# Attention scores issued as four 64x64 quarters of TensorE, with keys kept in half tiles

## The chip, the core and the metric

The kernel runs on one NeuronCore of one Trainium2 chip. The metric is the device time of one execution in microseconds (us). PE is the matrix engine TensorE, PEld its weight loads, DVE the vector engine, ACT the scalar engine, POOL the GpSimd engine and SP the engine whose queue issues nearly all DMAs. ns are nanoseconds.

## What is computed

An attention layer with a causal window of 128 keys, a token-mixing and channel-mixing layer, and a normalized feed-forward layer, for 4 sequences of 576 positions and 8 heads of 64. Cut to what the change touches:

```python
# B, H, S, D = 4, 8, 576, 64
scores = scale * np.matmul(q, k.transpose(0, 1, 3, 2))
rel = pos[:, None] - pos[None, :]
bias = slopes[:, None, None] * (-np.abs(rel))[None, :, :]
mask = (rel >= 0) & (rel < 128)
scores = np.where(mask, scores + bias[None], -1e9)
attn = softmax(scores)
x = attn @ v
# then, per sequence: u = x + (relu(x^T w_tok1) w_tok2)^T
#                     u = u + relu(u w_ch1) w_ch2
#                     out = u + relu(layernorm(u) w_ch1') w_ch2'
```

A query sees itself and the 127 keys before it. So a tile of 128 queries needs two tiles of keys, its own and the one before; 64 queries need only 192 keys.

## The kernel before

The 2304 positions are cut into 18 tiles of 128. Tile `i` may begin a sequence (tiles 0 and 9), and then it has one tile of keys; the 16 others have two. All operations are handed to `Plan.op` with a cost in ns for each engine that may run them, the tiles read and the tiles written. `Plan.order` (L205) is a list scheduler: it plays these costs through and fixes the order of every engine's instructions, SP's DMAs among them. A changed cost or an added operation can therefore move others, far from it.

**Attention (`attention`, L747).** In iteration `i` of the loop the block of `packed(i + 1, i - 1)` (L578) is issued on PE: first the scores of tile `i + 1`, in two parts `c` of four heads, then the products of the probabilities of tile `i - 1` with the values (`ps_v`, L608). The four parts are chained, so that nothing comes between them. Scores (L596) are fp32 matmuls: the stationary operand is 64 rows (one head's depth) of `q` by 128 queries, the moving one the 256 keys of the two key tiles. Heads come in pairs `j`, whose depths lie in partitions 0 to 63 and 64 to 127, and whose results go to two different PSUM banks of `ps_s`. Each fp32 matmul leaves two records in the trace, so a block of 8 score matmuls has 16 records; the 16 value matmuls have 32.

**Keys** lie in `keys`, a ring of RING = 4 tiles (L524); a load of 256 KB fills one (L532). For tiles whose place is the ring's first, the tile before is the ring's last, and `keys_of` (L563) gives a slice with a step that takes places 0 and 3 in turn, own keys first.

**Softmax (`softmax`, L623).** On DVE one `copy_predicated` (L631) of 128 x 512 takes, for each query, the older key's score wherever the own tile's key lies after the query, so that 128 columns are left of 256. Then four reductions (`CUSTOM_DVE_ANT_0`, L637) add the bias and find the minimum `mn`. ACT takes the exponentials (`pr`, L646), PE transposes them (`ps_t`, L653), ACT copies them to `pf` (L361), and POOL's `affine_select` (L663) splits them into the two key tiles. `normalize` (L667) has ACT copy `ps_v` to `ut`, PE transpose it and DVE scale it into `u[i]`.

**What runs beside it.** The token-mixing weights come as 64-bit floats through one buffer `rh` and two buffers `rw` (L404) and are made into fp32 pairs: `e` on ACT (L416), `s`, `m` and `y` on DVE (L419 to L431). `tok1` and `tok2` (L440 to L442, L735 to L737) are the token-mixing matmuls in three fp32r products each. They fill PE between the blocks. Near the end of attention `prep_wide` (L859) transposes `u` (`p`, L848) and lets DVE, ACT and POOL form sums and differences (`st`) and high and low halves (`xh`, `xl`) for the channel-mixing layer, whose first products are L993 to L995. From about 190 us on that layer and the next keep PE busy to the end.

Of the kernel before, what the change touches and what calls it, by code (L numbers as in the profile page):

```python
# [10 lines left out]
F32 = mybir.dt.float32  # L11
# [3 lines left out]
I32 = mybir.dt.int32  # L15
# [8 lines left out]
B, H, S, D = 4, 8, 576, 64  # L24
P = 128
DM = H * D
NT = B * S
NTILE = NT // P
# [4 lines left out]
RING = 4  # L33
# [69 lines left out]
class Plan:  # L103
# [22 lines left out]
    def buf(self, pool, shape, dtype, tag, bufs=1):  # L126
        b = Buf(self, pool, shape, dtype, tag, bufs)
        ring = self.rings.setdefault((pool, tag), [])
        if len(ring) >= bufs:
            b.after = [ring[-bufs]]  # L130
        if ring:
            b.behind = ring[-1]
        ring.append(b)
        return b
# [176 lines left out]
def pe(n):  # L311
    return 2.6 + n / 2.4


def block_kernel(tc, qT, kT, v, wt1, wt2, wa1, wa2, wb1, wb2, g, bias, out):
# [5 lines left out]
    def op(cost, emit, reads=(), writes=(), behind=()):  # L321
        return pl.op(cost, (lambda e: emit()) if len(cost) == 1 else emit, reads, writes, behind)
# [198 lines left out]
        return [buf("hid", [P, 2, S + P], F32R, "few" + p) for p in "hl"]  # L521


    keys = buf("att", [P, RING, H // 2, P], F32, "keys")  # L524
    wt1h, wt1l = ([buf("tok", [P, 5, TOK], F32R, f"wt1{x}{odd}") for odd in range(2)] for x in "hl")
    wt2h, wt2l = few()
    vs, qs = {}, {}
# [1 line left out]
    def load_qk(i):  # L529
        r = i % RING  # L530
        b = qs[i] = buf("att", [P, H // 2, P], F32, "q", Q_BUFS)
        op({"DMA": 1000}, lambda: nc.sync.dma_start(out=keys.t[:, r].rearrange("p h t -> p (h t)"), in_=kT[i]),  # L532
           writes=[(keys, r)])
        load(b, lambda: b.t.rearrange("p h t -> p (h t)"), P * DM * 4, qT[i])

    def load_v(i):
# [25 lines left out]

    def keys_of(i):  # L563

        s = i % RING
        if starts_batch(i):
            return [i], 0, 0, (s, s + 1, 1)
        table = 3 if len(batches_of(i)) > 1 else 2 if len(batches_of(i - 1)) > 1 else 1
        if s == 0:
            return [i, i - 1], 0, table, (0, RING, RING - 1)  # L570
        return [i - 1, i], 1, table, (s - 1, s + 1, 1)

    pv = buf("psb", [P, H // 2, P], F32, "ps_v")
    rs_t, xh_t, xl_t = {}, {}, {}
# [3 lines left out]
    def packed(i, i2):  # L578

        parts, ready = [], []
        if i is not None:
            tiles, own, table, (a0, a1, a2) = keys_of(i)
            w = len(tiles) * P
            x = qs[i]
            for c in range(2):
                ps_t[i, c] = buf("psa", [P, 2, 2, 2 * P], F32, "ps_s", 2)  # L590

                def scores(c=c, ps=ps_t[i, c]):
                    for p in range(2):
                        for j in range(2):
                            r = slice(j * D, (j + 1) * D)
                            nc.tensor.matmul(ps.t[:, j, p, :w], x.t[r, 2 * c + p], keys.t[r, a0:a1:a2, 2 * c + p],  # L596
                                             start=True, stop=True)

                parts.append((4 * pe(2 * w), scores, [x] + [(keys, t % RING) for t in tiles], [ps_t[i, c]]))
        if i2 is not None:  # L600
            tiles2 = keys_of(i2)[0]
            na = len(tiles2)
            for c in range(2):
                def values(c=c, pf=pf_t[i2, c]):
                    for p in range(2):
                        for a, kt in enumerate((i2, i2 - 1)[:na]):
                            for j in range(2):
                                nc.tensor.matmul(pv.t[j * D:(j + 1) * D, 2 * c + p], vs[kt].t[:, 4 * c + 2 * p + j],  # L608
                                                 pf.t[:, a, 2 * p + j], start=(a == 0), stop=(a == na - 1))

                parts.append((na * 440, values, [(pf_t[i2, c], a) for a in range(na)] + [vs[kt] for kt in tiles2],
                              [(pv, c)]))

        before = None
        for k, (cost, emit, reads, writes) in enumerate(parts):
            also = parts[k + 1:] if k == 0 else []
            now = op({"PE": cost + (200 if k in (0, len(parts) - 1) else 0)}, emit,
               reads + [x for p in also for x in p[2]], writes + [x for p in also for x in p[3]])
            if before is not None:
                pl.chain[before] = now  # L620
            before = now

    def softmax(i, c):  # L623

        tiles, own, table, _ = keys_of(i)
        na = len(tiles)
        ps = ps_t[i, c]
        o = slice(own * P, (own + 1) * P)
        if na == 2:
            b = slice((1 - own) * P, (2 - own) * P)  # L630
            op({"DVE": 690}, lambda: nc.vector.copy_predicated(  # L631
                ps.t[:, :, :, o], after.t.bitcast(I32).unsqueeze(1).unsqueeze(1).to_broadcast([P, 2, 2, P]),
                ps.t[:, :, :, b]), [ps, after], [ps])
        t = buf("att", [P, 4, P], F32, "t", T_BUFS)
        mn = buf("small", [P, 4], F32, "mn", 3)
        for m in range(4):
            op({"DVE": 358}, lambda m=m: nc.vector.tensor_tensor_reduce(  # L637
                out=t.t[:, m], in0=ps.t[:, m % 2, m // 2, o], in1=bias_sb.t[:, table, 4 * c + m],
                scale=-0.125, scalar=3.0e38, op0=ALU.add, op1=ALU.min, accum_out=mn.t[:, m:m + 1]),
               [ps, (bias_sb, table)], [(t, m), (mn, m)])  # L640
        pr = buf("att", [P, 4, P], F32, "pr", T_BUFS)
        if c == 0:
            rs_t[i] = buf("small", [P, H, 1], F32, "rs", 3)
        rs = rs_t[i]
        for m in range(4):
            op({"ACT": 580}, lambda m=m: nc.scalar.activation(  # L646
                out=pr.t[:, m], in_=t.t[:, m], func=AF.Exp, bias=mn.t[:, m:m + 1], scale=-1.0,
                accum_out=rs.t[:, 4 * c + m]), [(t, m), (mn, m)], [(pr, m), (rs, 4 * c + m)])
        pt = buf("psb", [P, 4, P], F32, "ps_t")

        def transposes():
            for m in range(4):
                nc.tensor.transpose(pt.t[:, m], pr.t[:, m], ident.t)  # L653

# [558 lines left out]
```

## Time and profile before

| | |
|---|---|
| time, median of 3 | 854.13 us (853.57 to 858.12) |
| the profiled execution | 856.19 us, of which its span is 854.5 us |
| PE busy in the span | 830.8 us (97%) |
| DVE busy | 638.1 us (75%) |
| ACT busy | 394.3 us (46%) |
| POOL busy | 338.5 us (40%) |
| DMA | 164.96 MB, mean 193 GB/s |

A row of a stretch gives the busy time of each engine with the number of its instructions, then the clock that TensorE was granted (1.00 is 2.4 GHz), the mean busy share of the 16 DMA engines and the rate. Matmuls overlap, and their ends are modelled, so that PE's busy time says less than the distances between the starts of its matmuls. A row of a timeline gives start, duration, engine, line, operation, the tile written and the tile read, the count, and in brackets the idle time before it and what ended that.

### The profile page before, as it was taken

The page shows a single profiled execution, that of the slowest core. Times are in us where ns is not written, and L with a number is a line of the kernel's source. Part 1 is how long each engine was busy: PE and PEld are TensorE (multiplying, and loading weights), DVE is VectorE, ACT ScalarE, POOL GpSimd, SP SyncE. Part 2 cuts the span into 40 slices and gives each one's busy share as a digit, 9 for nine tenths or more (in the row PEclk, how much of TensorE's full clock was granted, in tenths as well). Part 3 has the DMA queues.
Part 4 walks back from the last instruction along what each step waited for, and adds up shares of the span by engine and source line. Part 5 has one row for each costly group of instructions (what it writes and reads, how often), then busy time and mean ns, then how long its engine had stood idle before and what let it go on. Part 6 is the DMA issues. An engine that isn't in the chain of part 4 may idle for free.

```text
span 854.5 us, 13205 instructions
## 1 busy us (share of the span) xinstructions
PE 830.8 (97%) x4478; PEld 685.8 (80%) x4478; DVE 638.1 (75%) x1311; ACT 394.3 (46%) x952; POOL 338.5 (40%) x353
## 2 busy tenths in 40 slices
PE   7999999979999999999999999999999999999997
PEld 6777888758888887788887888788889888888885
DVE  5787777987887989987888956988676855555554
ACT  6888766643434535334357323336357422222220
POOL 2685445554433556532235524614234612221110
PEclk9999999999999999999999999999999999999999
DMA  8678736457677699978762521887477762221112
GB/s 296 187 207 265 242 103 213 146 179 241 200 234 240 228 324 337 348 252 268 264 210 74 178 92 48 264 263 258 154 259 234 247 198 74 74 75 49 50 50 98
DMA packets 73698, 164.96 MB, mean 193 GB/s; under 512 B 8352, under 2 KB 8480, under 8 KB 73632
## 3 DMA queue, kind: packets, MB, share of 16 engines
q1 hardware_dynamic: 73152, 162.83, 57.5%
q0 software_dynamic: 480, 1.31, 0.7%
q8 instruction: 35, 0.57, 0.3%
q14 instruction: 31, 0.25, 0.1%
HBM read 131.34 MB, written 31.46 MB: 191 GB/s over the span
## 4 chain that ended last, share of the span: by engine, by line
PE 83%; DVE 7%; ACT 4%; DMA 2%; issue 2%; POOL 1%; SPq 1%; ACTq 0%; DVEq 0%; POOLq 0%
PE acc L1048 12%; PE acc L1050 12%; PE acc L1049 12%; PE b L993 9%; PE b L995 9%; PE b L994 9%; PE ps_v L608 3%; PE ps_s L596 3%; PE p L848 1%; PE b L442 1%; PE b L441 1%; PE b L440 1%; PE ps_t L653 1%; DVE st L374 1%; PE tok L735 1%
## 5 line engine op out<-in xcount | busy, mean ns | idle before, releaser
L1053 DVE TENSOR_TENSOR u<-acc,u 128x512 f32<-128x512 f32 x252 | 172.9, 687 | 64.0 <-PE acc L1050 60.6
L1048 PE MATMUL acc<-w2h,hh 128*128 128x512 f32 x504 | 198.6, 394 | 5.3 <-DVE u L1053 4.7
L1050 PE MATMUL acc<-w2h,hl 128*128 128x512 f32 x504 | 196.6, 390 | 0.3 <-DVE hl L926 0.2
L1049 PE MATMUL acc<-w2l,hh 128*128 128x512 f32 x504 | 196.5, 390 | 0.0
L924 ACT ACTIVATE hh<-b 128x512 fp32r<-128x512 f32 (+1 forms) x140 | 74.5, 552 | 262.8 <-PE b L995 226.4
L993 PE MATMUL b<-xh,w1h 128*128 128x512 f32 x392 | 154.0, 393 | 3.6 <-DVE hl L926 3.4
L994 PE MATMUL b<-xl,w1h 128*128 128x512 f32 x392 | 153.3, 391 | 1.8 <-DVE xl L374 1.8
L995 PE MATMUL b<-xh,w1l 128*128 128x512 f32 x392 | 153.4, 391 | 0.2 <-DVE w1l L374 0.2
L926 DVE SCALAR_TENSOR_TENSOR hl<-b,hh 128x512 fp32r<-128x512 f32 (+1 forms) x140 | 85.8, 631 | 62.9 <-ACT hh L924 62.1
L374 POOL TENSOR_TENSOR w1l<-w,w1h 128x512 fp32r<-128x512 f32 (+1 forms) x53 | 67.6, 1275 | 134.0 <-ACT w1h L361 124.2
L1048 PEld LDWEIGHTS acc<-w2h,hh 128*128 128x128 f32 x504 | 94.7, 188 | 27.0 <-DVE u L1053 7.5
L1050 PEld LDWEIGHTS acc<-w2h,hl 128*128 128x128 f32 x504 | 94.6, 188 | 21.2 <-DVE hl L926 1.2
L1049 PEld LDWEIGHTS acc<-w2l,hh 128*128 128x128 f32 x504 | 94.7, 188 | 18.4
L374 POOL TENSOR_TENSOR w1l<-st,w1h 128x512 fp32r<-128x512 f32 x38 | 51.1, 1346 | 116.5 <-ACT w1h L361 103.2
L993 PEld LDWEIGHTS b<-xh,w1h 128*128 128x128 f32 x392 | 73.9, 189 | 19.8 <-DVE hl L926 3.8
L994 PEld LDWEIGHTS b<-xl,w1h 128*128 128x128 f32 x392 | 74.0, 189 | 17.4 <-DVE xl L374 2.3
L995 PEld LDWEIGHTS b<-xh,w1l 128*128 128x128 f32 x392 | 73.9, 189 | 16.1 <-DVE w1l L374 0.6
L416 ACT ACTIVATE e<-rh 128x512 bf16<-128x512 bf16 (+2 forms) x65 | 41.3, 635 | 74.0 <-DMA rh<-wb 33.6
L646 ACT ACTIVATE pr<-t,mn 128x128 f32<-128x128 f32 x144 | 55.9, 392 | 15.1 <-DVE mn L637 14.9
L663 POOL TENSOR_SCALAR_AFFINE_SELECT pf<-pf 128x512 f32<-128x512 f32 x64 | 42.3, 661 | 37.7 <-ACT pf L361 35.5
L374 DVE TENSOR_TENSOR b<-b,p 128x512 f32<-128x512 f32 x56 | 39.0, 697 | 23.6 <-PE b L995 23.1
L374 POOL TENSOR_TENSOR w2l<-w,w2h 128x512 fp32r<-128x512 f32 x23 | 32.1, 1395 | 46.1 <-ACT w2h L361 46.0
(118 smaller groups left out, 1369.3 us busy)
## 6 DMA issues: line engine op xcount, KB each, us to landing
w<-d SPq DMA_DIRECT2D x88, 256.0 KB, 4.6
rw<-wb SPq DMA_DIRECT2D x32, 512.0 KB, 4.5
rh<-wb SPq DMA_DIRECT2D x32, 512.0 KB, 4.7
rw<-wa SPq DMA_DIRECT2D x24, 512.0 KB, 4.5
rh<-wa SPq DMA_DIRECT2D x24, 512.0 KB, 4.5
d<-y SPq DMA_DIRECT2D x32, 256.0 KB, 4.4
keys<-kT SPq DMA_DIRECT2D x18, 256.0 KB, 4.3
q<-qT SPq DMA_DIRECT2D x18, 256.0 KB, 4.7
```

The source lines that it names most:

```text
L374: pl.op({e: cost[e] for e in on}, lambda e: ENGINE[e].tensor_tensor(get(), ga(), gb(), alu), [*several(a), *several(b), *also], several(dst))
L646: op({"ACT": 580}, lambda m=m: nc.scalar.activation(out=pr.t[:, m], in_=t.t[:, m], func=AF.Exp, bias=mn.t[:, m:m + 1], scale=-1.0, accum_o ...
L663: op({"POOL": 630}, lambda a=a: nc.gpsimd.affine_select(pf.t[:, a], pf.t[:, 1], [[0, 4], [1 - 2 * a, P]], (ALU.is_ge, ALU.is_gt)[a], 0.0, ...
L924: op({"ACT": act(n, True)}, lambda: nc.scalar.activation(out=hh.t[:, c], in_=go(), func=AF.Relu), [o], [(hh, key)])
L926: mark[0] = op({"DVE": dve(n)}, lambda: nc.vector.scalar_tensor_tensor(out=hl.t[:, c], in0=go(), scalar=0.0, in1=hh.t[:, c].bitcast(F32), ...
L993: nc.tensor.matmul(g.t, wh.t[:, w], xh.t, start=start and k == 0, stop=False, skip_group_check=True)
L994: nc.tensor.matmul(g.t, wh.t[:, w], xl.t, start=False, stop=False, skip_group_check=True)
L995: nc.tensor.matmul(g.t, wl.t[:, w], xh.t, start=False, stop=stop and k == 1, skip_group_check=True)
L1048: nc.tensor.matmul(o.t, hh.t[:, c:c + P], wh.t, start=j == 0, stop=False)
L1049: nc.tensor.matmul(o.t, hh.t[:, c:c + P], wl.t, start=False, stop=False)
L1050: nc.tensor.matmul(o.t, hl.t[:, c:c + P], wh.t, start=False, stop=j == 1)
L1053: op({"DVE": dve(DM)}, lambda o=o, i=i: nc.vector.tensor_tensor(u[i].t, o.t, u[i].t, ALU.add), [o], [u[i]])
```

## The change

- `keys` gets five places of two halves: `[P, (RING + 1) * 2, H // 2, D]`. Within a half the four head pairs lie one after the other, 64 keys each; the input `kT` is laid out on the host to match, so that a load is still 128 rows of 2 KB. A tile in ring place `r` goes to place `r + 1`; a tile with `r = 3` is loaded twice, to place 4 and to place 0. The tile before then always lies just ahead of the own one, and the own keys are always the second 128 columns of `ps_s`.
- Scores of a tile with two key tiles are issued as 16 matmuls instead of 8: for each head, the first 64 queries against keys 0 to 191 of the 256, the last 64 queries against keys 64 to 255. Each is 64 rows by 64 columns and 192 keys, and the four of a head pair write two halves of the partitions in two banks. Tiles with one key tile are issued as before.
- `copy_predicated` becomes two operations of 256 elements a partition: columns 64 to 127 for all 128 partitions, and columns 0 to 63 for partitions 0 to 63. What is left out is what the matmuls no longer write and the mask never takes.
- The costs told to the planner change: 4 * pe(192) * 2 for a part of the scores instead of 4 * pe(512), two operations of 430 instead of one of 690, and a further DMA of 1000 for each second load.

```diff
-    keys = buf("att", [P, RING, H // 2, P], F32, "keys")
+    keys = buf("att", [P, (RING + 1) * 2, H // 2, D], F32, "keys")
+
+    def span(r, h, first, n):
+        return keys.t[r, first // D:(first + n) // D, h]
...
-        op({"DMA": 1000}, lambda: nc.sync.dma_start(out=keys.t[:, r].rearrange("p h t -> p (h t)"), in_=kT[i]),
-           writes=[(keys, r)])
+        for j in (r + 1, 0) if r == RING - 1 else (r + 1,):
+            op({"DMA": 1000}, lambda j=j: nc.sync.dma_start(out=keys.t[:, 2 * j:2 * j + 2].rearrange("p a h t -> p (a h t)"), in_=kT[i]),
+               writes=[(keys, j)])
...
-                            nc.tensor.matmul(ps.t[:, j, p, :w], x.t[r, 2 * c + p], keys.t[r, a0:a1:a2, 2 * c + p],
-                                             start=True, stop=True)
-
-                parts.append((4 * pe(2 * w), scores, [x] + [(keys, t % RING) for t in tiles], [ps_t[i, c]]))
+                        for q in range(2):
+                            for j in range(2):
+                                r, m = slice(j * D, (j + 1) * D), slice(q * D, (q + 1) * D)
+                                nc.tensor.matmul(ps.t[m, j, p, q * D:q * D + 3 * D], x.t[r, 2 * c + p, m],
+                                                 span(r, 2 * c + p, a0 * P + q * D, 3 * D), start=True, stop=True)
+
+                parts.append((4 * pe(3 * D if w > P else P) * (2 if w > P else 1), scores,
+                              [x] + [(keys, k) for k in range(a0, a1)], [ps_t[i, c]]))
...
-            op({"DVE": 690}, lambda: nc.vector.copy_predicated(
-                ps.t[:, :, :, o], after.t.bitcast(I32).unsqueeze(1).unsqueeze(1).to_broadcast([P, 2, 2, P]),
-                ps.t[:, :, :, b]), [ps, after], [ps])
+            for rows, c0 in ((P, D), (D, 0)):
+                op({"DVE": 430}, lambda rows=rows, c0=c0: nc.vector.copy_predicated(
+                    ps.t[:rows, :, :, P + c0:P + c0 + D],
+                    after.t[:rows, c0:c0 + D].bitcast(I32).unsqueeze(1).unsqueeze(1).to_broadcast([rows, 2, 2, D]),
+                    ps.t[:rows, :, :, c0:c0 + D]), [ps, after], [ps])
```

SP, at the start of the kernel, from the load of the fourth tile's keys (the first row) to the first loads of token-mixing weights (`rh`, `rw`). Before:

```order
L532 DMA keys<-kT 128x512
L353 DMA v<-v 128x512
L353 DMA q<-qT 128x512
L353 DMA v<-v 128x512
L767 DMA bias_sb<-bias 128x2048
L404 DMA rh<-wt 128x2048
L532 DMA keys<-kT 128x512
L353 DMA q<-qT 128x512
L404 DMA rw<-wt 128x2048 x2
```

and after:

```order
L538 DMA keys<-kT 128x512
L353 DMA v<-v 128x512
L353 DMA q<-qT 128x512
L538 DMA keys<-kT 128x512
L353 DMA v<-v 128x512
L782 DMA bias_sb<-bias 128x2048
L538 DMA keys<-kT 128x512
L353 DMA q<-qT 128x512
L404 DMA rh<-wt 128x2048
L404 DMA rw<-wt 128x2048 x2
```

The fourth tile's second load of keys has come in, and the fifth tile's `keys` and `q` now stand ahead of the first `rh` instead of behind it: three DMAs more are ahead of it.

ACT, in the period whose first row starts at 43.39 us in the trace of before; `ut` is the copy that waits for the value matmuls, `pf` one that waits for the transposes. Before:

```order
L361 ACTIVATE xh<-u_669 128x512
L646 ACTIVATE pr,rs<-t,mn 128x128
L361 ACTIVATE ut<-ps_v 128x512
L361 ACTIVATE pf<-ps_t 128x512
L646 ACTIVATE pr,rs<-t,mn 128x128 x3
L361 ACTIVATE pf<-ps_t 128x512
```

and after:

```order
L361 ACTIVATE xh<-u_712 128x512
L361 ACTIVATE ut<-ps_v 128x512
L361 ACTIVATE pf<-ps_t 128x512
L661 ACTIVATE pr,rs<-t,mn 128x128 x2
L361 ACTIVATE pf<-ps_t 128x512
```

The one exponential that ran ahead of `ut` now runs behind the `pf` that follows it.

DVE, between two tiles in the same part of the program. Before:

```order
L431 SCALAR_TENSOR_TENSOR y<-m,s 128x256
L423 TENSOR_SCALAR m<-rw 128x256
L631 COPY_PREDICATED ps_s<-after,ps_s 128x4x128 x2
L637 ISA t,mn<-ps_s,bias_sb 128x128
L637 ISA mn 128x1
```

and after:

```order
L431 SCALAR_TENSOR_TENSOR y<-m,s 128x256
L423 TENSOR_SCALAR m<-rw 128x256
L645 COPY_PREDICATED ps_s<-after,ps_s 128x4x64 x2
L645 COPY_PREDICATED ps_s<-after,ps_s 64x4x64 x2
L652 ISA t,mn<-ps_s,bias_sb 128x128
L652 ISA mn 128x1
```

The four copies of a tile stand as first, first, second, second of the two parts `c`, all ahead of the first reduction; the second copy of the first part stands behind a copy that waits for the second part.

## Rows read from the trace of the kernel before

**Rows 1.** Stretches: busy us and instructions of each engine, clock, DMA share, GB/s.

```profile
10.00:20.00 10.00, 7.23 (x56) 5.21 (x58) 7.22 (x40) 8.87 (x37) 3.05 (x6) 0.95 0.90 339
20.00:30.00 10.00, 9.89 (x90) 7.65 (x90) 7.18 (x29) 7.56 (x27) 5.75 (x10) 0.88 0.63 163
40.00:50.00 10.00, 9.85 (x85) 7.54 (x86) 7.43 (x29) 8.76 (x36) 5.99 (x9) 1.00 0.50 157
70.00:80.00 10.00, 9.59 (x100) 7.54 (x97) 8.18 (x41) 9.01 (x34) 4.22 (x7) 1.00 0.81 264
100.00:110.00 10.00, 10.00 (x102) 8.12 (x100) 7.74 (x27) 8.16 (x26) 6.45 (x8) 1.00 0.58 185
160.00:170.00 10.00, 9.43 (x45) 7.84 (x46) 10.00 (x16) 5.63 (x12) 4.43 (x4) 1.00 0.57 184
170.00:180.00 10.00, 6.73 (x29) 4.55 (x27) 9.76 (x13) 5.97 (x11) 9.18 (x9) 1.00 0.30 78
```

**Rows 2.** Chain that ended last: start us, us, what.

```profile
9.28 5.94 DMA rh<-wt
15.68 0.49 ACT ut L361
...
19.24 3.46 PE ps_s L596 x16
...
82.49 1.93 PE ps_s L596 x16
...
125.88 1.93 PE ps_s L596 x16
```

**Rows 3.** Timeline of PE through one block of scores and values.

```profile
106.88 2.00 PE L596 MATMUL ps_s<-keys,q 64*128 64x256 f32 x16
108.81 1.97 PE L608 MATMUL ps_v<-pf,v 128*64 128x128 f32 x32
110.70 0.66 PE L653 MATMUL ps_t<-ident,pr 128*128 128x128 f32 x4
111.11 0.49 PE L735 MATMUL tok<-hh,fewh 128*128 128x512 f32 x1
```

**Rows 4.** Instructions on ps_s and ps_v: durations ns min/median/max, first and last start, forms.

```profile
L596 PE MATMUL ps_s<-keys,q x288: 272/376/792, 5.6 to 127.4; 64*128 64x256 f32 x128, 64*128 64x128 f32 x16
...
L608 PEld LDWEIGHTS ps_v<-pf,v x544: 132/137/137, 13.1 to 146.7; 128*64 128x64 f32 x182
```

**Rows 5.** Timeline of SP's queue at the start.

```profile
8.59 0.33 SPq L767 DMA_DIRECT2D bias_sb<-bias  x1
9.28 0.33 SPq L404 DMA_DIRECT2D rh<-wt  x1
10.00 0.33 SPq L532 DMA_DIRECT2D keys<-kT  x1
10.64 0.33 SPq L353 DMA_DIRECT2D q<-qT  x1
11.31 1.01 SPq L404 DMA_DIRECT2D rw<-wt  x2
```

**Rows 6.** Timeline of ACT, at the start and in one later period.

```profile
15.25 0.43 ACT L416 ACTIVATE e<-rh 128x256 bf16<-128x256 bf16 x1 [1.14 <-DMA rh<-wt]
...
43.39 0.63 ACT L361 ACTIVATE xh<-u 128x512 fp32r<-128x512 f32 x1
44.64 0.40 ACT L646 ACTIVATE pr<-t,mn 128x128 f32<-128x128 f32 x1 [0.61 <-DVE mn L637]
44.95 0.19 ACT L646 ACTIVATION_READ_ACCUMULATOR pr<-t,mn 128x1 f32 x1
45.55 0.60 ACT L361 ACTIVATE ut<-ps_v 128x512 f32<-128x512 f32 x1 [0.41 <-PE ps_v L608]
```

**Rows 7.** Timeline of DVE: a copy of 512 elements, an operation of 256.

```profile
126.53 0.42 DVE L421 SCALAR_TENSOR_TENSOR s<-e,s 128x256 int32<-128x256 int32 x1
126.86 0.20 DVE L680 RECIPROCAL rc<-rc 128x8 f32<-128x8 f32 x1
...
127.60 0.42 DVE L423 TENSOR_SCALAR m<-rw 128x512 uint32<-128x512 uint32 x1
127.93 0.28 DVE L637 CUSTOM_DVE_ANT_0 t<-ps_s,bias_sb 128x128 f32<-128x128 f32 x1
...
128.77 0.69 DVE L631 COPY_PREDICATED ps_s<-after,ps_s 128x512 f32<-128x512 int32 x1
129.37 0.69 DVE L431 SCALAR_TENSOR_TENSOR w<-m,s 128x512 f32<-128x512 uint32 x1
```

**Rows 8.** PE's longest waits on DVE at the end of attention, from its timeline.

```profile
174.34 0.50 PE L994 MATMUL b<-xl,w1h 128*128 128x512 f32 x1 [1.84 <-DVE xl L374]
182.09 0.50 PE L993 MATMUL b<-xh,w1h 128*128 128x512 f32 x1 [3.36 <-DVE hl L926]
```

More of the change, by code (lines that the diff above doesn't have):

```diff
@@ L563, in keys_of @@
     def keys_of(i):
-        s = i % RING
         if starts_batch(i):
[L567 to L571, printed above, removed]
+            return [i], 0
+        return [i - 1, i], 3 if len(batches_of(i)) > 1 else 2 if len(batches_of(i - 1)) > 1 else 1
     pv = buf("psb", [P, H // 2, P], F32, "ps_v")
@@ L585, in packed @@
         if i is not None:
-            tiles, own, table, (a0, a1, a2) = keys_of(i)
-            w = len(tiles) * P
+            tiles, table = keys_of(i)
+            a1 = i % RING + 2
+            a0, w = a1 - len(tiles), len(tiles) * P
             x = qs[i]
@@ L593, in scores @@
                     for p in range(2):
-                        for j in range(2):
-                            r = slice(j * D, (j + 1) * D)
-                            nc.tensor.matmul(ps.t[:, j, p, :w], x.t[r, 2 * c + p], keys.t[r, a0:a1:a2, 2 * c + p],
-                                             start=True, stop=True)
-                parts.append((4 * pe(2 * w), scores, [x] + [(keys, t % RING) for t in tiles], [ps_t[i, c]]))
+                        if len(tiles) == 1:
+                            for j in range(2):
+                                r = slice(j * D, (j + 1) * D)
+                                nc.tensor.matmul(ps.t[:, j, p, :w], x.t[r, 2 * c + p], span(r, 2 * c + p, a0 * P, w),
+                                                 start=True, stop=True)
+                            continue
+                        for q in range(2):
+                            for j in range(2):
+                                r, m = slice(j * D, (j + 1) * D), slice(q * D, (q + 1) * D)
[3 more added lines that the diff above has]
+                              [x] + [(keys, k) for k in range(a0, a1)], [ps_t[i, c]]))
         if i2 is not None:
@@ L623, in softmax @@
     def softmax(i, c):
-        tiles, own, table, _ = keys_of(i)
+        tiles, table = keys_of(i)
         na = len(tiles)
+        own = na - 1
         ps = ps_t[i, c]
@@ L629, in softmax @@
         if na == 2:
-            b = slice((1 - own) * P, (2 - own) * P)
-            op({"DVE": 690}, lambda: nc.vector.copy_predicated(
-                ps.t[:, :, :, o], after.t.bitcast(I32).unsqueeze(1).unsqueeze(1).to_broadcast([P, 2, 2, P]),
-                ps.t[:, :, :, b]), [ps, after], [ps])
+            for rows, c0 in ((P, D), (D, 0)):
[3 more added lines that the diff above has]
+                    ps.t[:rows, :, :, c0:c0 + D]), [ps, after], [ps])
         t = buf("att", [P, 4, P], F32, "t", T_BUFS)
@@ L1186 @@
         arrays[f"{n}T"] = np.ascontiguousarray(a.transpose(3, 1, 2, 0, 4)).reshape(NTILE, P, DM)
+    arrays["kT"] = np.ascontiguousarray(arrays["kT"].reshape(NTILE, P, H // 2, 2, D).swapaxes(2, 3)).reshape(NTILE, P, DM)
     arrays["v"] = np.ascontiguousarray(x["v"].transpose(0, 2, 1, 3)).reshape(NT, DM)
```

## The prediction

> **What bounds the kernel now.** I read the table of stretches first, to find what limits each stage, then the chain that ended last, then the timelines of PE, SP, ACT and DVE at the places that the change touches. The change touches only attention, so what counts is how much earlier or later the channel-mixing matmuls begin, from which PE runs without a gap to the end.
>
> There are four stages. At the start ACT and the DMAs are busiest: from 10 to 20 us ACT is busy 8.87 of 10 us, the DMAs 0.90, PE 7.23 [rows 1]. The chain runs through a load there: `rh` is issued at 9.28 us and lands 5.94 us later, and behind it comes ACT's `ut` [rows 2], because `e`, which needs `rh`, stands ahead of `ut` on ACT and made it wait 1.14 us [rows 6]. From about 25 to 80 us ACT is at 8.8 to 9.0 of 10, and PE shows 9.6 to 9.9 [rows 1], but a record of PE is longer than its distance to the next one (2.00 us against 1.93 in [rows 3]), so short waits of PE are hidden in it. ACT's own waits show who paces whom: in one period it waits 0.61 us for DVE's minima and 0.41 us for the value matmuls [rows 6]. From about 82 to 126 us PE is busy 10.00 of 10 [rows 1] and the score blocks lie whole on the chain: the first at 82.49, the last at 125.88 us, 1.93 us each, six in number [rows 2]. From 150 to 182 us DVE is the bound, at 9.8 to 10.0 of 10 us [rows 1], and PE waits for it, 1.84 and 3.36 us in its two longest [rows 8].
>
> **A block of scores.** Before, 16 records of 256 keys take 1.93 us from the block's start to the next block's, and the 32 records of 128 columns in the value block take 1.89 us [rows 3]. A lone record of 128 columns takes 0.10 us (four transposes, 110.70 to 111.11, [rows 3]). One at a time, 32 of them would take 3.3 us, so the value records run two at a time, in two column halves; 16 of 256 would take the same 3.3, so the score records run two at a time as well, in two row halves. With a step for each pair: 16 steps of 128 columns in 1.89 us and 8 steps of 256 in 1.93 us. If both blocks begin and end alike, about 0.15 us goes to that, and a step takes 0.109 us for 128 columns and 0.22 us for 256; for 192 I take 0.163 us, in between.
>
> After, a tile with two key tiles has 32 records of 192 keys. The trace has pairs of rows and pairs of columns, but nothing in four quarters. If four run at once, there are 8 steps of 0.163 us, 1.30, and 0.15 us around them: 1.45 us, **0.48 us less a block**. If the four don't start together and one step is lost to that, it is 0.32 us less. If only two run at once, there are 16 steps: 2.61 + 0.15 = 2.76 us, 0.83 us more. I take four: row halves and column halves each work without loss, and nothing in the rows ties one to the other. There are 128 score matmuls with 256 keys [rows 4], so 16 such tiles.
>
> A rule of the Trainium skill speaks against this. The value block has 32 weight loads of 0.137 us [rows 4] whose matmuls all use the same 128 rows; its 16 steps, with the two column halves loading side by side, would be 0.137 us longer each if loads could not run under matmuls, 4.1 us in all, and it takes 1.89 [rows 3]. The Trainium skill, TensorE: Matmul & The Clock Gate, Part 3 (Packing small matmuls), says that a weight load overlaps running matmuls only where their row groups differ. By that rule each of the 8 new steps would carry its load, 8 x 0.137 = 1.10 us, and the block would be 0.62 us longer instead of shorter. The trace does not agree with it for the value block.
>
> **What 0.48 us is worth, stage by stage.** *82 to 126 us:* six blocks on the chain with PE full, so 6 x 0.48 = 2.9 us less (1.9 with a step lost). *25 to 80 us:* seven tiles with two key tiles. Here ACT decides. In the period of [rows 6], ACT is done with `xh` at 44.02, does one exponential after a wait, and `ut` starts at 45.55. After, `ut` comes first: the value block ends 0.48 us earlier, so `ut` starts at 45.07, but the exponential, about 0.39 us of ACT, is still to be done. That leaves about 0.1 us, and the minima don't come earlier: the last scores are there 0.48 us earlier, but after them DVE now has three short copies ahead of the first reduction instead of one long one (3 x 0.33 against 0.60 us, see below), 0.4 us more. What follows `ut` on PE (its transposes, `u`) gains a little more. I take 0.2 us a tile, 7 x 0.2 = 1.4 us less; the ends are 0 and 7 x 0.48 = 3.4. *Before 25 us* three blocks wait for loads and ACT; I count nothing.
>
> **The copies on DVE.** One of 512 elements occupies DVE for 0.60 us (128.77 to 129.37), an operation of 256 for 0.33 us (126.53 to 126.86) [rows 7]. Two of 256 are 0.07 us more than one of 512, 32 x 0.07 = 2.2 us in attention. Where a second copy must wait until the first is quite finished (0.42 us, not 0.33, [rows 7]), it is 0.16 us, 5.1 us in all; the interleaved order avoids that for most. DVE is idle for 1.8 to 2.8 of 10 us from 20 to 110 us [rows 1], which covers either. After attention DVE is the bound, and the order gives it about one operation `m` of 512 more to do there, 0.33 us [rows 7] or up to twice that beside POOL: 0.5 us more.
>
> **The second loads of keys.** Four more DMAs of 256 KB. Three of them fall into stretches with DMAs at 0.5 to 0.8 [rows 1], behind which the planner has moved `e` on ACT; I count nothing. The first falls into the start, where the DMAs are at 0.90 [rows 1] and SP issues one about every 0.65 us as older ones land (8.59, 9.28, 10.00, 10.64, 11.31, [rows 5]). In the order, three DMAs more stand ahead of the first `rh` than before: the second load, and `keys` and `q` of the fifth tile. So `rh` goes out where the first `rw` did, at 11.31 instead of 9.28 us, and lands **2.0 us** later; all but 0.3 us of the queue ahead of it is as long as before. `e` has kept its place on ACT, ahead of `ut`, so ACT's wait grows from 1.14 to about 3.1 us, and that is on the chain [rows 2]. It could be hidden if the chain has slack further on (0), or cost more: the block at 19.24 took 3.46 us instead of 1.93 [rows 2], where the granted clock falls to 0.88 of full on average [rows 1] after a stretch with PE waiting; another block at the 1.2 GHz level would add 1.5 us. I take 2.0, between 0 and 3.5.
>
> **The sum:** + 2.0 (start) - 1.4 (25 to 80 us) - 2.9 (82 to 126 us) + 0.5 (DVE after attention) = - 1.8 us. The profiled execution took 856.19 us and would take 854.4; it lies 2.1 us above the median of 854.13, and I apply the difference to that: **852.3 us**. Bounds: - 6.3 (0, - 3.4, - 2.9, 0) gives 847.8, and + 2.4 (3.5, 0, - 1.9, 0.8) gives 856.5.
>
> **The rivals.**
> *The whole gain arrives, chance 0.22.* ACT's late `e` is made good within the first periods, and the blocks before 80 us count in full: the lower bound, 847.8. For it: PE's part of a period shrinks, and ACT still has over 1 us of idle time in each of 10 [rows 1]. Against it: the exponentials are only moved behind `ut`.
> *Quarters run two at a time, chance 0.07.* The change does not do what it says: 16 x 0.83 = 13.3 us more, and 2 at the start, 869; if ACT hides it before 80 us, only 6 x 0.83 = 5.0 and 2: 861. It decides as soon as a block takes over 1.93 us.
> *Weight loads show, chance 0.03.* By the mechanism priced above: 16 x 0.62 = 9.9 and 2, 866. This is what the rule of TensorE: Matmul & The Clock Gate in the Trainium skill would give.
> *DVE becomes the bound of attention, chance 0.12.* The copies wait for each other, 5.1 us, and attention, shorter by some 4 us, leaves DVE no idle time to put them in; DVE then enters the stage at 150 us late, and PE waits longer there [rows 8]: 2.0 + 5.1 - 1.4 = 5.7 us more, 859.8. It decides if DVE's idle time before 126 us, 2 of 10 us now, falls towards none.
>
> **How the numbers follow.** The forecast, a small gain, has 0.56. A difference of 0.5%, 4.3 us, is about what a measurement of this kernel can tell from no change (its runs spread from 853.57 to 858.12). Faster by more than that, below 849.9: the first rival, mostly, and a little of the forecast's lower side, 0.24. Slower, above 858.4: the last three, 0.22 in all. Within: 0.54. Leaving out most of the two matmul rivals and the outermost part of the first, the range is 847.5 to 860.
>
> **What would show it.** Score blocks of 1.45 us from start to start of the value block show four at a time; 1.61 a lost step; 2.55 exposed loads; 2.76 pairs. ACT's first `e` after a wait of about 3 us on `rh` shows the cost at the start. Six blocks on the chain from 80 us on show where the gain is paid. The first copies to `st` and `xl` at the end of attention, and PE's waits on DVE there, show if the gain survives. I would be wrong if the new order of DVE, POOL and ACT between 130 and 190 us, which I cost at 0.5 us only, moves the start of channel mixing by several us.

## The result, and the profile after

| | before | after |
|---|---|---|
| median of 20 runs | 853.82 us (851.42 to 858.12) | 859.66 us (854.93 to 862.17) |
| the profiled execution, and its span | 856.19 us, 854.5 us | 859.22 us, 857.5 us |

After / before is 1.0063, 95% interval 1.0052 to 1.0074: the change makes the kernel **slower by 0.63%, 5.4 us**. The prediction was 852.3 us. The measured time lies just inside its range, but on the other side of no change.

The table of stretches of the changed kernel, with the columns of [rows 1]:

```profile
10.00:20.00 10.00, 5.32 (x66) 3.55 (x64) 5.41 (x34) 6.68 (x28) 1.12 (x3) 1.00 0.97 351
20.00:30.00 10.00, 9.21 (x81) 7.11 (x82) 6.77 (x35) 6.80 (x27) 6.36 (x10) 0.66 0.52 155
40.00:50.00 10.00, 9.64 (x113) 7.36 (x110) 8.01 (x45) 8.21 (x29) 6.98 (x11) 1.00 0.68 231
70.00:80.00 10.00, 5.92 (x65) 4.50 (x65) 5.56 (x27) 7.51 (x26) 5.77 (x7) 0.83 0.63 218
100.00:110.00 10.00, 10.00 (x104) 8.37 (x102) 7.57 (x38) 7.63 (x25) 7.23 (x9) 1.00 0.60 177
```

Two stretches answer badly to [rows 1]. From 10 to 20 us PE has 5.32 us of work instead of 7.23, and in the next 10 us the granted clock is 0.66 on average instead of 0.88. From 70 to 80 us PE has 5.92 us instead of 9.59. From 100 to 110 us PE is as full as before.

The chain that ended last, to 79 us (start us, us, what):

```profile
5.02 6.94 DMA keys<-kT
11.97 5.89 DMA rh<-wt
...
21.92 2.77 PE ps_s L607 x32
24.69 3.05 PE ps_v L620 x32
...
30.47 1.46 PE ps_s L607 x32
31.93 1.92 PE ps_v L620 x32
...
61.64 8.82 DMA rh<-wt
...
76.86 2.11 PE ps_s L607 x32
```

Against [rows 2], the chain now runs through two loads of `rh` instead of one, the first at the start and the second at 61.64 us. Behind the first stands a score block that takes 2.77 us instead of 1.46, and behind the second one that takes 2.11. Where PE was not disturbed before, the block is what the prediction wanted: the timeline of PE,

```profile
105.68 1.53 PE L607 MATMUL ps_s<-keys,q 64*64 64x192 f32 x32
107.14 1.53 PE L620 MATMUL ps_v<-pf,v 128*64 128x128 f32 x24
```

has 1.46 us from the block's start to the value block's start, against 1.93 in [rows 3]: **0.466 us less**, and four quarters run at once. Eleven of the 16 blocks take 1.461 us.

SP's queue at the start, beside [rows 5], and ACT's two waits for `rh`, beside [rows 6]:

```profile
9.93 0.33 SPq L782 DMA_DIRECT2D bias_sb<-bias  x1
10.66 0.33 SPq L538 DMA_DIRECT2D keys<-kT  x1
11.29 0.33 SPq L353 DMA_DIRECT2D q<-qT  x1
11.97 0.33 SPq L404 DMA_DIRECT2D rh<-wt  x1
12.64 1.00 SPq L404 DMA_DIRECT2D rw<-wt  x2
```

```profile
17.88 0.43 ACT L416 ACTIVATE e<-rh 128x256 bf16<-128x256 bf16 x1 [3.32 <-DMA rh<-wt]
18.22 0.58 ACT L361 ACTIVATE ut<-ps_v 128x512 f32<-128x512 f32 x1
...
66.51 0.19 ACT L661 ACTIVATION_READ_ACCUMULATOR pr<-t,mn 128x1 f32 x1
70.57 0.46 ACT L416 ACTIVATE e<-rh 128x288 bf16<-128x288 bf16 x1 [3.87 <-DMA rh<-wt]
70.93 0.58 ACT L727 ACTIVATE hh<-tok 128x512 fp32r<-128x512 f32 x1
71.40 0.43 ACT L361 ACTIVATE fewh<-y 128x288 fp32r<-128x288 f32 x1
71.74 0.59 ACT L361 ACTIVATE pf<-ps_t 128x512 f32<-128x512 f32 x1
...
73.50 0.59 ACT L361 ACTIVATE ut<-ps_v 128x512 f32<-128x512 f32 x1
```

The first wait was in the prediction: 3.32 us, after about 3.1 expected. The second, 3.87 us at 70.57, was not. Before, the `e` of the same load (the eighth of `rh`) began at 70.60 without waiting:

```profile
66.86 0.58 ACT L361 ACTIVATE ut<-ps_v 128x512 f32<-128x512 f32 x1
...
70.51 0.20 ACT L646 ACTIVATION_READ_ACCUMULATOR pr<-t,mn 128x1 f32 x1
70.60 0.47 ACT L416 ACTIVATE e<-rh 128x288 bf16<-128x288 bf16 x1
```

The `ut` at 73.50 after and at 66.86 before is that of tile 7: `e` stands ahead of it after the change and behind it before. `hh` and `fewh` (high halves of token-mixing products and weights) and `pf`, which PE needs, are queued behind `e` after the change. On PE both waits are seen a moment later, as idle time before the transposes of `ut` (timeline of PE):

```profile
18.85 0.66 PE L690 MATMUL ps_v<-ident,ut 128*128 128x128 f32 x4 [3.78 <-ACT ut L361]
...
21.85 2.84 PE L607 MATMUL ps_s<-keys,q 64*64 64x192 f32 x32
...
74.14 0.66 PE L690 MATMUL ps_v<-ident,ut 128*128 128x128 f32 x4 [4.08 <-ACT ut L361]
...
76.79 2.18 PE L607 MATMUL ps_s<-keys,q 64*64 64x192 f32 x32
```

The time at which `u` of each tile is scaled on DVE places the loss. Counting tiles from 0, after against the profile of before: tile 0 + 2.2 us, tile 2 + 2.7, tile 6 + 0.2, **tile 8 + 8.6**, tile 14 + 4.4, tile 17 + 4.6; the end of PE's work + 3.7. (The profiled execution of before was itself 2.4 us above its median.) So three things happen: a loss at the start, a loss of 8.4 us between tiles 6 and 8, and a gain in the stretches between (2.4 us from tile 2 to tile 6, 4.2 us from tile 8 to tile 14).

### The profile page after: what moved, and what is told of

It reads as the page before. It is cut to its first block, busy times and chain, and to the rows that moved or that the text cites. A ratio compares the mean times of both kernels' runs of the same rounds, so it can differ in the third digit from the quotient of the medians.

```text
span 857.5 us, 13744 instructions
## 1 busy us (share of the span) xinstructions
PE 828.6 (97%) x4734; PEld 683.8 (80%) x4734; DVE 637.6 (74%) x1344; ACT 392.8 (46%) x952; POOL 337.3 (39%) x352
## 4 chain that ended last, share of the span: by engine, by line
PE 83%; DVE 7%; ACT 4%; DMA 3%; issue 2%; POOL 1%; SPq 0%; ACTq 0%; DVEq 0%
PE acc L1063 12%; PE acc L1065 12%; PE acc L1064 12%; PE b L1009 10%; PE b L1008 10%; PE b L1010 10%; PE ps_v L620 3%; PE ps_s L607 2%; DMA rh<-wt 2%; DVE st L374 1%; PE p L863 1%; PE b L442 1%; PE b L441 1%; PE b L440 1%; PE ps_t L668 1%
## 5 line engine op out<-in xcount | busy, mean ns | idle before, releaser
L1063 PE MATMUL acc<-w2h,hh 128*128 128x512 f32 x504 | 198.4, 394 | 5.3 <-DVE u L1068 4.7
L1008 PE MATMUL b<-xh,w1h 128*128 128x512 f32 x392 | 154.1, 393 | 0.2 <-DVE b L374 0.2
L374 POOL TENSOR_TENSOR w1l<-w,w1h 128x512 fp32r<-128x512 f32 (+1 forms) x54 | 69.5, 1289 | 132.8 <-ACT w1h L361 123.9
L1063 PEld LDWEIGHTS acc<-w2h,hh 128*128 128x128 f32 x504 | 94.7, 188 | 27.2 <-DVE u L1068 7.5
L1008 PEld LDWEIGHTS b<-xh,w1h 128*128 128x128 f32 x392 | 74.2, 189 | 16.3 <-DVE b L374 0.9
L1010 PEld LDWEIGHTS b<-xh,w1l 128*128 128x128 f32 x392 | 74.3, 190 | 15.5
```

The lines of the kernel that those rows point to most:

```text
L374: pl.op({e: cost[e] for e in on}, lambda e: ENGINE[e].tensor_tensor(get(), ga(), gb(), alu), [*several(a), *several(b), *also], several(dst))
L1008: nc.tensor.matmul(g.t, wh.t[:, w], xh.t, start=start and k == 0, stop=False, skip_group_check=True)
L1010: nc.tensor.matmul(g.t, wl.t[:, w], xh.t, start=False, stop=stop and k == 1, skip_group_check=True)
L1063: nc.tensor.matmul(o.t, hh.t[:, c:c + P], wh.t, start=j == 0, stop=False)
```

## The experiments

Each ratio is to the kernel before in runs on the same chip; the changed kernel's is 1.0063.

### First: the second loads, the copies, the planner's costs

Theory A held the second loads of keys, and through them the late `rh`, to be the loss; theory B the copies on DVE and the new order that the new costs give.

**no_dups**: the changed kernel with the four-place ring of before and no second loads. The first 64 queries' 192 keys of a tile in ring place 0 are then cut into two matmuls.

```diff
-        for j in (r + 1, 0) if r == RING - 1 else (r + 1,):
+        for j in (r,):
...
-                                nc.tensor.matmul(ps.t[m, j, p, q * D:q * D + 3 * D], ...)
+                                pieces = [(q * D, 3 * D)] if a0 >= 0 else [(q * D, P - q * D), (P, D + q * D)]
+                                for o, n in pieces:
+                                    nc.tensor.matmul(ps.t[m, j, p, o:o + n], ...)
```

> Quarters as in the changed kernel, but no second loads: the ring keeps its four places, and for the four tiles whose own keys lie in place 0 each matmul of 192 keys is cut in two pieces (128 and 64 keys). Theory A, the second loads delay the token-mixing weights (rh), and ACT and PE wait for them: the first e on ACT starts near 15.3 us as before instead of 17.9, its waits for rh stay under 2 us, and the time is 847 to 850 us, 4 to 7 below the kernel before. Theory B, the new order or the split copies cost the time: 857 to 860 us as the changed kernel.

Measured: 852.09 us, ratio 0.9979 [0.9966, 0.9992]. `rh` is issued at 10.00 us again, ACT's first `e` waits 1.61 us, and the loss is gone. The gain, 0.2%, is still far from what 16 blocks of 0.466 us would be, and the time lies between the ranges of the two theories.

**loads_only**: the kernel before with a second load of the same four tiles into an added place. No matmul reads it; the planner is told that the next tile's scores need it.

```diff
-        op({"DMA": 1000}, lambda: nc.sync.dma_start(out=keys.t[:, r]..., in_=kT[i]), writes=[(keys, r)])
+        for j in (r, RING) if r == RING - 1 else (r,):
+            op({"DMA": 1000}, lambda j=j: nc.sync.dma_start(out=keys.t[:, j]..., in_=kT[i]), writes=[(keys, j)])
```

> The kernel before with one thing added: the tiles in the ring's last place are loaded a second time, into a fifth place that no matmul reads (the planner is told that the scores of the next tile need it, so that it is queued as in the changed kernel). Theory A: the first e at 17.5 to 18 us, and the time 4 to 9 us above the kernel before, 857 to 863. Theory B: within 1.5 us of the kernel before.

Measured: 858.7 us, ratio 1.0057 [1.0035, 1.0079]. The first `rh` is issued at 11.51 us, ACT waits,

```profile
17.47 0.43 ACT L416 ACTIVATE e<-rh 128x256 bf16<-128x256 bf16 x1 [3.11 <-DMA rh<-wt]
```

and `u` of tile 0 is 2.7 us later than before. It is still 2.7 us later at tiles 2, 6, 8, 14 and 17: nothing in attention makes good what is lost at the start. The time and the wait are what theory A expected. The second stall does not appear: the eighth `e`, at 73.32 us, waits for nothing here.

**copies_only**: the kernel before with the copy of 512 elements cut into the two of 256.

```diff
-            op({"DVE": 690}, lambda: nc.vector.copy_predicated(ps.t[:, :, :, o], ...))
+            for rows, c0 in ((P, D), (D, 0)):
+                op({"DVE": 430}, lambda rows=rows, c0=c0: nc.vector.copy_predicated(
+                    ps.t[:rows, :, :, own * P + c0:own * P + c0 + D], ...))
```

> The kernel before with only the predicated copy split in two, of 256 elements each. Theory A: within 1.5 us of the kernel before, since DVE has idle time in attention (0.07 us more a part of a tile, 2.2 us in all). Theory B, the copies hold up softmax: 3 to 6 us above it.

Measured: 854.22 us, ratio 1.0003 [0.999, 1.0017]. The copies cost nothing.

**old_costs**: the changed kernel, but the planner is told the costs of before (the sum of two copies 690, the score parts as with 256 keys, nothing for a load into place 0).

```diff
-            op({"DMA": 1000}, ...
+            op({"DMA": 1000 if j else 0}, ...
-                parts.append((4 * pe(3 * D if w > P else P) * (2 if w > P else 1), scores,
+                parts.append((4 * pe(2 * w), scores,
-                op({"DVE": 430}, lambda rows=rows, c0=c0: nc.vector.copy_predicated(
+                op({"DVE": 345}, lambda rows=rows, c0=c0: nc.vector.copy_predicated(
```

> The changed kernel, with the planner told the costs of before (scores as two heads at 256 keys, the two copies together 690, nothing for the load into place 0), so that the order is close to that of before; at the start rh has one load more ahead of it than before, not three. Theory A: the wait for the first rh grows by 0.7 to 1 us instead of 2.6, the later ones may stay; 850 to 857 us. Theory B, the new order of ACT, DVE and POOL is the cause: 848 to 851.

Measured: 851.78 us, ratio 0.9983 [0.9969, 0.9997]. All four second loads are there, yet `rh` goes out ahead of the fifth tile's `keys` and `q`, at 9.98 us, and ACT waits 1.24 us. The time lies in the range of A and just above that of B, but ACT's wait grew by 0.1 us where A wanted 0.7 to 1. So it is neither the transfers by themselves (A as it stood) nor the copies (the one half of B): it is the **order** that the new costs give (the other half of B). That `rh` and `e` are what counts in it is argued here from the traces; the next runs test it.

### Second: where `e` stands on ACT

Theory C: what is lost is ACT standing still in its order behind an `e` whose `rh` is late. Theory D: the loss is in the order elsewhere, in the transition to channel mixing above all. The planner was told that a load of `rh` lands 4 us later than it reckons; it then puts the `e` of that load further back on ACT. Nothing else is edited:

```diff
-                    ready[j] = max(ready[j], free[e] + self.lat(...) if k in ops[j][2] else at + 1)
+                    ready[j] = max(ready[j], free[e] + self.extra.get(k, 0) + self.lat(...) if k in ops[j][2] else at + 1)
...
+        pl.nth += 1
+        pl.extra[first] = {1: 4000, 8: 4000}.get(pl.nth, 0)
```

The number in front of 4000 says which load of `rh` is meant; one such entry is called a word below. **after_late** is the changed kernel with both words, **before_late** the kernel before with them, as a control.

> The changed kernel, second loads and all, with the planner told that the first and the eighth load of rh land 4 us later than it assumes, so that the first e stands behind a tile's exponentials on ACT. Theory C (the loss of the changed kernel is ACT standing still behind late loads of rh): ACT waits under 1 us for rh in all, 849 to 853 us, below the kernel before. Theory D (the second loads cost time in other ways, DMA bandwidth or the keys themselves): 856 to 860.

> Control: the kernel before with the same two words to the planner. Its first e waited 1.1 us and its eighth not at all, so theory C gives 852 to 854 us (1 us less at most). If it gains 3 us or more, the two words help by something else than the waits seen.

Measured: after_late 847.37 us, ratio 0.992 [0.9898, 0.9941], **faster than both kernels**; before_late 855.35 us, ratio 1.0006 [0.9992, 1.002]. The words alone bring nothing in the kernel before. after_late is 1.6 us below the range of theory C; its ACT waits 1.1 us for token-mixing loads of `rh`, and 2.4 us more for a later load. `u` of tile 0 comes 3.7 us earlier than in the changed kernel, of tile 8 13.1 us earlier.

**no_dups_late** and **no_dups_late8** are no_dups with both words, and with that for the eighth load alone (`{8: 4000}`).

> Quarters, no second loads, first and eighth rh told late. Theory C: 847 to 850 us; the difference to before_late is the worth of the quarters alone, 3 to 5 us. Theory D: within 2 us of before_late.

> The kernel with quarters and without second loads (no_dups, 852.1 us), with the planner told that the eighth load of token-mixing weights (rh) lands 4 us later than it assumes; that moves the eighth e on ACT behind the next tile's exponentials. In no_dups ACT waited 1.5 us there after reaching it early, with a tile's exponentials queued behind it, and 4 us of the 6 gained by then were lost between 59 and 76 us. Theory C, that stall is where the gain of the quarters goes: 848 to 850 us, u of the ninth tile (u8) 3 us or more earlier than in no_dups. Theory D, the gain is lost to DVE in the transition whatever happens before: 851.5 to 853.

Measured: 852.06 us, ratio 0.9968 [0.9953, 0.9983], and 852.59 us, ratio 0.9984 [0.9966, 1.0001]. Here theory C in its simple form fails: neither is better than no_dups by much, and neither time is in its range. Only the difference of no_dups_late to before_late, 3.3 us by the medians, lies in the 3 to 5 that it gave to the quarters. In no_dups_late8 tiles 6 to 8 are 2.8 us quicker than in no_dups (14.0 against 16.8 us), as C wanted, but at the start its granted clock is at the 1.2 GHz level for longer and takes 1.5 us of that back by tile 2. In no_dups_late, ACT has the same order as in after_late and still waits 5.2 us for token-mixing loads of `rh` (1.1 there). Why its loads land later although there are fewer of them is open.

### Third: the two stalls one at a time

**after_late1** and **after_late8** are the changed kernel with one word each (`{1: 4000}`, `{8: 4000}`). Theory F: one stall hides the other. Theory G: neither word alone helps.

> The changed kernel, with only the first of the two words to the planner: the first rh load lands 4 us later, so that e of the start stands behind the first value block's ut on ACT; the eighth load as before. Theory C (each stall of ACT behind a late rh costs its own time): the two words together brought 859.7 - 847.4 = 12.3 us, of which 8.4 us were there by the seventh tile's u; so the start is worth about 8.4 us and this kernel takes about 851, and it still loses about 4 us between the seventh and the ninth u if e waits there for rh by over 2 us. Rival F (one stall hides the other, so that either word alone brings the whole): 847 to 849. Rival G (the order as a whole is what counts, and neither word alone helps): 857 to 861.

> The changed kernel, with only the second word: the eighth rh load lands 4 us later, so that its e stands behind the exponentials of the tile on ACT; the start as in the changed kernel, with its first e waiting about 3 us for rh and u of the first tile 2 us late. Theory C: what the second stall costs comes back, 12.3 - 8.4 = about 4 us, so about 856, with the stretch from the seventh to the ninth u 4 us shorter than in the changed kernel (16.7 instead of 20.7 us). Rival F (one stall hides the other): 847 to 849. Rival G (neither word alone helps): 857 to 861.

Measured: after_late1 **846.56 us, ratio 0.9909** [0.9881, 0.9936]; after_late8 855.85 us, ratio 1.0005 [0.9989, 1.002]. The second is about what theory C said: removing the second stall gives 3.8 us by the medians, 5.0 by the ratios, and the eighth `e` waits for nothing. The stretch from tile 6 to tile 8 is still 3.1 us longer than before (15.5 us against 12.3), with TensorE at the lower clock for 3.4 us of it. The first is what F said, but not for F's reason. In the trace of after_late1 ACT waits for none of the nine token-mixing loads of `rh`. ACT's timeline there, at the start and at the eighth `e`:

```profile
14.19 0.58 ACT L362 ACTIVATE ut<-ps_v 128x512 f32<-128x512 f32 x1
...
59.94 0.57 ACT L362 ACTIVATE ut<-ps_v 128x512 f32<-128x512 f32 x1
...
63.30 0.47 ACT L419 ACTIVATE e<-rh 128x288 bf16<-128x288 bf16 x1
```

The `ut` at 59.94 is tile 7's. The first word, put in for the start, also moved the eighth `e` from ahead of that `ut` to behind it, where it stands before the change; and its `rh`, issued at 57.90, took 4.75 us instead of 8.82. So that run took both stalls away, and 9.3 us, the rest of its 13.1, is no price of the start alone. The stretches at the start and at the second stall, of after_late1:

```profile
10.00:20.00 10.00, 8.39 (x116) 6.01 (x118) 7.38 (x45) 10.00 (x42) 3.86 (x8) 1.00 0.95 352
20.00:30.00 10.00, 9.44 (x116) 7.24 (x112) 8.58 (x47) 9.05 (x36) 7.24 (x11) 1.00 0.82 265
...
70.00:80.00 10.00, 10.00 (x132) 8.26 (x125) 8.81 (x48) 8.32 (x29) 5.06 (x9) 1.00 0.87 287
```

ACT is busy 10.00 of 10 us at the start (6.68 in the changed kernel), PE 8.39 (5.32), and the clock stays at full speed. `ut`, which waited until 18.22, runs at 14.19.

### Fourth: what the quarters are worth

**wide_after** is the changed kernel, **wide_after_late1** is after_late1, each with the scores issued as before, 8 matmuls of 256 keys; the costs told to the planner and the order of ACT, DVE, POOL and SP stay. So the difference is the score blocks alone.

```diff
-                        if len(tiles) == 1:
+                        if True:
                             for j in range(2):
                                 r = slice(j * D, (j + 1) * D)
                                 nc.tensor.matmul(ps.t[:, j, p, :w], x.t[r, 2 * c + p], span(r, 2 * c + p, a0 * P, w), ...)
```

> The changed kernel, but the scores of tiles with two key tiles are issued as before, in 8 matmuls of 128 queries and 256 keys (a block of 1.93 us instead of 1.46); second loads, half copies and the costs told to the planner stay, and so does the order of ACT, DVE, POOL and SP. Against the changed kernel (859.7) this gives what the quarters are worth in its own order. The prediction's terms (1.4 before 80 us, 2.9 after): 864. Full worth (16 x 0.466 = 7.5): 867. Nothing, because the waits of ACT for rh hide them all: 860; hidden only in and before the two stretches with late loads, 4.2 us shown: 864 too, but then all of it behind 80 us.

> The changed kernel with the first word to the planner (e of the start behind ut, 846.6), and the scores issued as before, in 8 matmuls of 256 keys; all else and the order of ACT, DVE, POOL and SP as there. With no wait for rh left, theory C wants the quarters' full worth here: 846.6 + 7.5 = 854. By the prediction's terms, 0.2 a tile before 80 us and full behind: 846.6 + 4.3 = 851. If the gain of 846.6 over before was the order's and not the quarters': 847 to 848.

Measured: wide_after 863.6 us, ratio 1.0113 [1.0091, 1.0136]; wide_after_late1 851.68 us, ratio 0.9961 [0.9948, 0.9975]. PE's timeline of wide_after shows the old block, 1.92 us from start to start:

```profile
107.61 2.00 PE L600 MATMUL ps_s<-keys,q 64*128 64x256 f32 x16
109.53 1.97 PE L620 MATMUL ps_v<-pf,v 128*64 128x128 f32 x32
```

In the changed kernel's order the quarters bring 863.6 - 859.66 = 3.9 us, or 4.3 us by the two ratios; the prediction's terms gave 4.3. In the order without stalls they bring 5.1 us by the medians and 4.4 by the ratios. That is more than nothing and less than the full 7.5, so theory C's "full worth" fails as well. (The two profiled executions of that order are 6.7 us apart, but the one of after_late1 lies 1.1 us below its median.) By the intervals of the ratios, each of these two differences is uncertain by 2 to 3 us either way. Some of the quarters' worth goes into longer waits: in wide_after ACT's two waits for `rh` are 2.76 and 2.98 us, in the changed kernel 3.32 and 3.87. What is left for the order, the second loads and the half copies together is wide_after against before, **1.13%, 9.6 us**. The order of after_late1 takes 12 us back (863.6 - 851.68), which is all of it and more: with the old score blocks it is 0.4% faster than the kernel before. So not all that the first word brings is the end of a stall.

## Why the prediction was wrong

**A block of scores: right.** 1.461 us against 1.45, four quarters at once. No weight load shows: the rival with exposed loads wanted 2.55 us. That is what the rule of the Trainium skill (TensorE: Matmul & The Clock Gate, Part 3, Packing small matmuls) would give as the prediction priced it. This block does not agree with it. The rows of the tile, in which the loads' durations (min/median/max, ns) stand beside the matmuls', are those of 32 loads and 32 records a block, in two row groups:

```profile
L607 PEld LDWEIGHTS ps_s<-keys,q x512: 129/133/228, 8.0 to 131.9; 64*64 64x64 f32 x171
L607 PE MATMUL ps_s<-keys,q x512: 322/323/579, 8.1 to 132.1; 64*64 64x192 f32 x171
```

**What the gain is worth: right, as far as the runs can tell.** - 1.4 and - 2.9 us were predicted; wide_after gives 3.9 to 4.3 in all, uncertain by about 2 us. By the times of `u`, the changed kernel gains on wide_after 1.1 us from tile 2 to tile 6 and 2.7 us from tile 8 to tile 14. The estimate of 0.2 us a tile in the first part, which was chosen between 0 and 0.48, holds in size.

**The copies on DVE: right.** copies_only shows no cost. In the timeline of DVE the last of the four copies is done 1.1 us after the last scores, as reckoned:

```profile
106.63 0.43 DVE L645 COPY_PREDICATED ps_s<-after,ps_s 128x256 f32<-128x256 int32 x1 [1.18 <-PE ps_s L607]
107.28 1.08 DVE L645 COPY_PREDICATED ps_s<-after,ps_s 128x256 f32<-128x256 int32 x3 [0.22 <-PE ps_s L607]
108.28 0.28 DVE L652 CUSTOM_DVE_ANT_0 t<-ps_s,bias_sb 128x128 f32<-128x128 f32 x1
```

The rival in which DVE becomes the bound did not come; its forecast of 859.8 us fits the time by chance.

**The transition: right enough.** From `u` of tile 17 to the first products with the second channel-mixing weights (`acc`, L1048 before and L1063 after) the changed kernel takes 40.5 us, against 41.2 before. The first product of channel mixing itself (L993, L1008 after) starts 7.8 us later than before, at 172.94 instead of 165.15 us, but at the first `acc` it is 3.9 us. The place that the prediction named as its greatest risk moved by under 1 us against `u` of tile 17.

**The start: mechanism right, too small.** The first `rh` was late by 2.7 us (11.97 against 9.28), `u` of tile 0 by 2.2. The prediction took 2.0 between 0 and 3.5. After PE's wait of 3.78 us the clock is granted at half. The stretches:

```profile
20.00:27.00 7.00, 6.32 (x59) 4.82 (x61) 5.63 (x28) 4.56 (x18) 5.43 (x8) 0.51 0.49 143
27.00:30.00 3.00, 2.89 (x27) 2.28 (x24) 1.13 (x8) 2.24 (x9) 0.93 (x2) 1.00 0.57 183
```

A clock of 0.51 is the 1.2 GHz level nearly throughout, and both the score block and the value block lie in it (2.77 and 3.05 us against 1.46 and 1.92, 2.4 us more). In before one score block lay at the lower level [rows 2]. loads_only measures the second loads by themselves, in the order of before, at + 0.57%, 4.9 us (3.0 to 6.7 by its interval): the term was too small, and its upper end was the better value. Its profile against that of before shows 2.7 us from tile 0 to tile 17, and in the transition 2.6 us the other way, so that the 4.9 us rest on the runs' times and not on these two traces.

**The later loads: the step that failed.** The prediction set the other three second loads to nothing ("I count nothing"), because they fall into stretches with DMAs at 0.5 to 0.8, "behind which the planner has moved `e` on ACT". That was read from the rows of [rows 1] and from the order in one period, and not from every `e` with the load ahead of it. [rows 1] has no row from 60 to 70 us, at whose start one of these three loads goes out (59.76 us, below). There the DMAs were at 1.07 even in the kernel before:

```profile
60.00:70.00 10.00, 9.02 (x90) 7.03 (x88) 8.11 (x41) 8.85 (x37) 7.20 (x12) 1.00 1.07 257
```

The place of `e` was misjudged too. The new costs, with cheaper scores and the half copies, moved the eighth `e` the wrong way, by nearly a tile: before, it stands behind the `ut` of tile 7 (66.86 us), and ACT's turn comes to it 11.1 us after its `rh` was issued (59.46); after, it stands ahead of that `ut` (73.50), and the turn comes at 66.70, 5.1 us after the issue. Its `rh` at the same time came later and took longer. SP's queue before, and after:

```profile
59.46 0.84 SPq L404 DMA_DIRECT2D rh<-wt  x1
```

```profile
59.39 0.33 SPq L353 DMA_DIRECT2D q<-qT  x1
59.76 1.38 SPq L538 DMA_DIRECT2D keys<-kT  x1
61.64 0.33 SPq L404 DMA_DIRECT2D rh<-wt  x1
```

The second load of a tile's keys (59.76) stands just ahead of `rh`, which goes out at 61.64 instead of 59.46 us and takes 8.82 us, where the same load took 5.8 before. ACT stands still for 3.87 us, PE for 4.08, and the next score block lies for the most part at half the clock. The stretch from tile 6 to tile 8 takes 20.7 us instead of 12.3, 8.4 us more, where the sum had 0.4 less. Taking this `e` out of the way brings 3.8 to 5.0 us (after_late8). Not all of the 8.4 us reaches the end, since later tiles catch up: between tiles 8 and 14 the changed kernel gains 4.2 us on before, of which the quarters make 2.7.

Put together: the quarters brought what was predicted, - 4.3 us. The order, the second loads and the half copies cost 9.6 us, where the sum had + 2.5 (2.0 and 0.5). Both stalls are one mechanism, a load of `rh` that lands after ACT's turn for `e`; the prediction priced it once, too low, and missed it the second time. How the 9.6 us divide is not settled. The first stall alone, in the order of before, costs 4.9 us (loads_only); the second, with the first in place, costs 3.8 to 5.0 (after_late8). Together that is 8.7 to 9.9 us, which fits, but the two numbers come from different orders, and no run removed the first stall alone from the changed kernel.

## What to carry to other kernels

When a planner sets the order, list for every operation that waits for a DMA which DMAs have come in ahead of it and what is queued behind it on its in-order engine, before and after; a look at one typical period is not enough. Here cheaper matmuls moved such an operation forward, and a load that had been in time was late. Telling the planner a pessimistic landing time for those loads, and trying the old and the new costs, are cheap things to try. Here one number, 4 us of lateness for the first load, turned + 0.63% into - 0.91% (846.56 us, the fastest of the kernels run). It is no sure remedy: in no_dups and in the kernel before, the two words changed the time by about 0.1%.

## What the hardware showed that was not expected

- Fp32 matmuls of 64 rows by 64 columns and 192 keys ran four at a time with next to no loss: 32 records in 1.461 us, where three quarters of the 1.93 us of the old block would be 1.45, with 32 weight loads of 0.133 us under them.
- The waits of PE cost more than their length here. 3.78 us of waiting at 15 to 19 us were followed by about 6.8 us at the 1.2 GHz level; PE was busy 6.32 of 7 us there, with a granted clock of 0.51. What follows does not go by the length of the wait alone: 4.08 us of waiting at 70 to 74 us were followed by 3.4 us at that level.
- The same load of 288 KB took 8.82 us in the changed kernel and 4.75 us in after_late1, issued at 61.64 and at 57.90 us. The DMAs' mean busy share is 1.12 in the 10 us from 60 us on, and 0.97 at the start, where 256 KB took 5.89 us. The share does not explain the slow load: it was 1.14 during the 8.82 us, and 1.08 during the 4.75 us of after_late1. By the time of the packets nearly half of the traffic at the slow load is not SP's. What exactly holds it up was not tried. The row of the stretch, and from 60 to 71 us the two main queues (packets, MB, share of 16 engines); q0 carries the DMAs that POOL issues:

```profile
60.00:70.00 10.00, 8.58 (x95) 6.35 (x89) 5.51 (x26) 5.60 (x21) 6.51 (x11) 1.00 1.12 246
```

```profile
q1 hardware_dynamic: 884, 1.76, 60.1%
q0 software_dynamic: 437, 1.09, 50.6%
```
